# Sorted attention and expert layer: v sorted ahead of k, and the load of q heads 4 to 7 moved behind the k sort

## The chip, the cores and the metric

The kernel runs on one core of one Trainium2 chip. The metric is the device time of one execution in microseconds (us). A profile gives the span of the program on the core, about 2 us less than the device time. Ratios below come from runs of both kernels on the same chip, in the same rounds.

## The reference, cut to what matters

```python
P = sort_net                                   # [4, 8, 8, 8], five Sinkhorn steps
for _ in range(5):
    P = exp(P - max(P)); P = P / sum(P, -1); P = P / sum(P, -2)
k_sorted = einsum('bhij,bhjcd->bhicd', P, k_blocks)      # "sort" of k and v: 8 blocks mixed by P
v_sorted = einsum('bhij,bhjcd->bhicd', P, v_blocks)
attn = softmax(q_block @ k_sorted_block.T / 8)           # within each of the 8 blocks of 96
x = (attn @ v_sorted_block)                              # -> [3072, 512]
e = argmax(x @ w_gate + modality_bias)                   # one expert of 8 for each row
out = gate * (relu(x @ w1[e]) @ w2[e])
```

q, k and v are [4, 8, 768, 64] in fp32; the expert weights are [8, 512, 1024] and [8, 1024, 512].

## The kernel before

The 32 pairs of batch and head are worked in two groups of 16 pairs of rows. For each group k and v are brought to SBUF (GpSimd issues these loads, they cast fp32 to bf16), mixed by a 128 x 128 block matrix `bd` on TensorE (the sorts), and evacuated (copied out of TensorE's output buffers) by ScalarE and VectorE. q is loaded, *spread* (a copy that interleaves two heads), and transposed on TensorE. 32 units then follow, each with scores, exp and the product with v. Behind units 0 to 7 the rows go through a gate and are *scattered* by expert into a scratch table in HBM, and from unit 16 on the first expert's matmuls are mixed in, which read the scratch table through a transposed load (`xT`).

The loads at the start, in GpSimd's program order:

```python
load_q(0, 0, 2)
...                                   # cut: iota, identity
load_k(0, 0)
load_k(0, 1)
load_v(0)
load_q(0, 2, 2)
load_q(0, 4, 4)
...                                   # cut: constants
spread_q(0, 0, nc.gpsimd)
```

and the first group's sorts:

```python
kinds = [s_] + [m_] * 4 + [o_] + [m_] * 4 + ([m_] * 4 + [o_]) * 2 + [m_] * 4
g0 = jobs(0, kinds)                   # 10 jobs of k, then 14 of v
for f, g, x0, kd in g0[:10]:
    f(g, x0, kd)
load_k(1, 0)
load_k(1, 1)
home_map()                            # VectorE, then GpSimd: which expert is "home"
spread_q(0, 1, nc.gpsimd)             # q heads 2 and 3
gate_w()
for n, (f, g, x0, kd) in enumerate(g0[10:]):
    f(g, x0, kd)
    ...                               # cut: scores of units 0 and 1 in between
load_v(1)
spread_q(0, 2, nc.gpsimd)             # q heads 4 and 5
gate_bias()
prep_q(2); av(0); prep_q(3)
spread_q(0, 3, nc.gpsimd)             # q heads 6 and 7
load_q(1, 0, 4)
load_w(0, parts=(0,))
load_q(1, 4, 4)
load_w(0, parts=(1,))                 # last bulk load ahead of the experts
```

What an expert's first matmul stands on: eight scatters of `place(0)`, then the transposed load.

```python
ins = nc.gpsimd.indirect_dma_start(out=xs_dram, ..., in_=xt[:, t])       # 8 times, one queue
i1 = nc.sync.dma_start_transpose(out=xT_b[s % NX], in_=view)             # waits for all 8
nc.tensor.matmul(hp[:, f], w_at(...), xT_b[s % NX][:, c], ...)           # mL1
```

The softmax here doesn't subtract the row's maximum and nothing guards it: scores larger than these inputs give would overflow.

## Time and profile before

| | before |
|---|---|
| device time, median of the first 3 runs | 188.99 us (188.81 to 190.06) |
| span of the profile | 186.9 us |
| TensorE busy | 160.0 us, 86% |
| last packet of the bulk loads ends | 61.61 us |
| first expert matmul (`hp`) starts | 69.33 us |
| from there to the end | 117.6 us |

How to read it: the page's slices show which resource is full at what time, the chain of waits shows what released each step, the timeline gives single instructions with the idle time in front of them in brackets. Lines such as L365 are lines of the kernel; the changed kernel's are one or two lower. The packet times in this document are from the trace's record of DMA packets.

### The profile page before, as it was taken

Reading aid. Unit: us, or ns where it says so; the run is one execution under the profiler, and the core shown is the slowest. Engines: PE = TensorE matmul, PEld = TensorE weight load, DVE = VectorE, ACT = ScalarE, POOL = GpSimd, SP = SyncE. Lnnn points to the kernel's source line nnn. Section 1 sums busy time; section 2 is a strip of 40 time slices with the busy share of each in tenths; the row PEclk is TensorE's granted clock in tenths of the full one; section 3 lists DMA queues with packets and bytes.
Section 4 is the critical chain, followed back from the end, with each engine's and each line's share of the span. In section 5 each row is a group of like instructions: output and inputs, shape, how many; then the busy total and the mean of one; then the engine's idle time right before and its main releaser. Section 6 shows DMA issues by size and latency. Waiting matters only on the chain.

```text
span 186.9 us, 5311 instructions
## 1 busy us (share of the span) xinstructions
PE 160.0 (86%) x2116; PEld 121.0 (65%) x2127; DVE 101.5 (54%) x334; ACT 91.5 (49%) x147; POOL 83.7 (45%) x118
## 2 busy tenths in 40 slices
PE   6495597888499978999899999999999995999980
PEld 6484496766388966767648867658666664676430
DVE  4878677975557967848694657014723223132321
ACT  3134577766759875956467724532422321223120
POOL 7921288970085204455507744676522322206232
PEclk9969999999858999999999999999999999999999
DMA  3999999999999534999219532797469852002311
GB/s 45 208 217 210 193 211 216 224 206 218 211 203 221 159 60 64 189 184 287 70 26 123 186 102 77 128 242 192 132 129 202 169 145 71 24 36 109 119 56 56
DMA packets 30161, 27.67 MB, mean 148 GB/s; under 512 B 18831, under 2 KB 25775, under 8 KB 29872
## 3 DMA queue, kind: packets, MB, share of 16 engines
q0 software_dynamic: 11792, 23.10, 55.8%
q1 hardware_dynamic: 18336, 4.16, 14.0%
q8 instruction: 18, 0.29, 0.7%
q14 instruction: 15, 0.12, 0.2%
HBM read 27.35 MB, written 10.52 MB: 203 GB/s over the span
## 4 chain that ended last, share of the span: by engine, by line
PE 35%; DMA 23%; issue 21%; POOL 9%; DVE 8%; POOLq 2%; SPq 0%; DVEq 0%
PE hp L690 11%; DMA out_dram<-kvb,idg 11%; PE yp L713 9%; DMA kvb<-in_v_dram 9%; POOL xs_scratch L534 4%; POOL out_dram L704 4%; PE va L374 3%; PE op L436 3%; DVE xb L444 3%; PE gt L453 2%; PE sc L417 2%; PE lg L463 2%; DMA xs_scratch<-xb,dest 2%; DMA xT<-xs_scratch 2%; DVE v_sb L352 1%
## 5 line engine op out<-in xcount | busy, mean ns | idle before, releaser
L690 PE MATMUL hp<-xT,w 128*128 128x256 bf16 x384 | 46.4, 273 | 1.5 <-DMA xT<-xs_scratch 1.4
L534 POOL DMA_INDIRECT xs_scratch<-xb,dest x32 | 29.5, 922 | 34.4 <-issue 27.5
L704 POOL DMA_INDIRECT out_dram<-kvb,idg x25 | 24.6, 985 | 43.0 <-DVE kvb L702 16.8
L690 PEld LDWEIGHTS <-w 128*128 128x128 bf16 x384 | 36.3, 98 | 9.5 <-issue 1.4
L423 ACT ACTIVATE attnT<-sc 96x768 bf16<-96x768 f32 x32 | 25.9, 810 | 7.7 <-PE sc L417 7.3
L713 PE MATMUL yp<-w,hT 128*128 128x512 bf16 x90 | 21.9, 379 | 2.2 <-PEq L1009 1.9
L444 DVE TENSOR_TENSOR xb<-op,rs 96x512 bf16<-96x512 f32 x32 | 22.0, 686 | 1.1
L713 PE MATMUL yp<-w,qT 128*128 128x512 bf16 x91 | 22.3, 379 | 0.3
L700 ACT ACTIVATE kvb<-yp,idg 128x512 f32<-128x512 f32 x14 | 9.6, 687 | 22.9 <-PE yp L713 22.9
L702 DVE TENSOR_SCALAR kvb<-yp,idg 128x512 f32<-128x512 f32 x10 | 7.5, 751 | 20.0 <-PE yp L713 18.1
L713 PEld LDWEIGHTS <-hT 128*128 128x128 bf16 x96 | 9.0, 98 | 11.2 <-issue 2.1
L436 PE MATMUL op<-v_sb,attnT 96*128 96x65 bf16 x256 | 13.6, 197 | 2.9 <-DVE xb L444 2.4
L684 ACT ACTIVATE hT<-hp 128x512 bf16<-128x512 f32 x18 | 10.7, 596 | 10.8 <-PE hp L690 10.3
L684 ACT ACTIVATE qT<-hp 128x512 bf16<-128x512 f32 x16 | 9.3, 594 | 12.8 <-PE hp L690 12.2
L713 PEld LDWEIGHTS <-qT 128*128 128x128 bf16 x96 | 9.0, 98 | 9.3
L374 PE MATMUL va<-bd,kvb 128*128 128x128 bf16 x128 | 13.2, 261 | 1.5 <-DMA kvb<-in_v_dram 1.5
L374 PEld LDWEIGHTS <-kvb 128*128 128x128 bf16 x128 | 12.4, 200 | 1.7 <-DMA kvb<-in_v_dram 1.6
L352 ACT CAST kT<-ka 128x512 bf16<-128x512 f32 (+1 forms) x17 | 9.9, 640 | 6.9 <-PE ka L365 6.9
L436 PEld LDWEIGHTS <-attnT 96*128 96x128 bf16 x256 | 10.7, 100 | 3.9 <-DVE xb L444 2.8
L242 ACT COPY qT<-tq 128x768 bf16<-128x768 bf16 x14 | 11.1, 794 | 3.6 <-PE tq L236 3.5
L352 ACT CAST v_sb<-va 96x512 bf16<-96x512 f32 (+1 forms) x19 | 10.9, 613 | 3.8 <-PE va L374 3.4
L682 DVE TENSOR_SCALAR hT<-hp 128x512 bf16<-128x512 f32 x6 | 4.1, 692 | 14.4 <-PE hp L690 13.3
(182 smaller groups left out, 227.3 us busy)
## 6 DMA issues: line engine op xcount, KB each, us to landing
w<-in_moe_w_dram POOLq DMA_DIRECT2D x4, 1024.0 KB
kvb<-in_k_dram POOLq DMA_DIRECT2D x4, 768.0 KB
kvb<-in_v_dram POOLq DMA_DIRECT2D x2, 1536.0 KB
q_in<-in_q_dram POOLq DMA_DIRECT2D x4, 384.0 KB
xs_scratch<-zpad SPq DMA_DIRECT2D x3, 258.0 KB, 3.2
v_sb<-in_q_dram POOLq DMA_DIRECT2D x4, 192.0 KB
v_sb<-in_q_dram POOLq DMA_DIRECT2D x2, 384.0 KB
xs_scratch<-xb,dest POOLq DMA_INDIRECT x32
```

The costliest lines, as they stand in the source:

```text
L242: eng(qT, tq.pop(u).rearrange("p t (i r) -> p i t r", r=16))
L352: (nc.scalar.copy if pick(act, dve) else nc.vector.tensor_copy)(dst, src)
L374: nc.tensor.matmul(acc[:, z], v_cols[:, d0 + z], bd[g], start=True, stop=True)
L423: mark[0] = nc.scalar.activation(attnT[u % 2][:, 0:8 * BLK].rearrange("p (r f) -> p r f", r=2), sc_tiles.pop(u)[0:BLK, :, 0:4 * BLK], ACT. ...
L436: nc.tensor.matmul(ov[:, par, j], attnT[u % 2][:, c0:c0 + 128], v_sb[g][0:BLK, par * 64 + h * 8 + i, 0:D + 1], start=True, stop=True)
L444: nc.vector.tensor_tensor(xt[:, :, h * D:(h + 1) * D].rearrange("p (r j) d -> p r j d", r=2), ov[0:BLK, :, :, 0:D], rs.broadcast_to([BLK, ...
L534: ins = nc.gpsimd.indirect_dma_start(out=xs_dram, out_offset=bass.IndirectOffsetOnAxis(ap=dest[:, t:t + 1], axis=0), in_=xt.bitcast(I32)[: ...
L684: mark[0] = nc.scalar.activation(dst, src, ACT.Relu)
L690: nc.tensor.matmul(hp[:, f], w_at(s, c * F + (2 * j + f) * 128, 128), xT_b[s % NX][:, c], start=(c == 0), stop=(c == 3))
L700: nc.scalar.activation(dst, src, ACT.Copy, scale=gate)
L704: ins = nc.gpsimd.indirect_dma_start(out=out, out_offset=bass.IndirectOffsetOnAxis(ap=idg[:, t, 0:1], axis=0), in_=y, in_offset=None, boun ...
L713: nc.tensor.matmul(yp, hT_b[s % 2][:, fc, t * 128:(t + 1) * 128], w_at(s, 4 * F + fc * Dm, Dm), start=(fc == 0), stop=(fc == 7))
```

## The change

Intent: k lands early and v late, so that TensorE sorts k, pauses, and waits 1.5 us for v. With v first, the wide v matmuls run while k is still landing. The load of q heads 4 to 7 and the second group's loads are to go out only when the k sort is nearly over, so that no bulk load is under way there, and the spreads of heads 4 to 7 move to VectorE.

```diff
     load_q(0, 0, 2)
+    load_v(0)
     load_k(0, 0)
     load_k(0, 1)
-    load_v(0)
     load_q(0, 2, 2)
-    load_q(0, 4, 4)
 ...
+    for f, g, x0, kd in g0[10:]:
+        f(g, x0, kd)
+    home_map()
+    spread_q(0, 1, nc.gpsimd)
     for f, g, x0, kd in g0[:10]:
         f(g, x0, kd)
-    (second k loads, home_map, spread of heads 2 and 3, gate_w, v sort with scores 0 and 1 inside)
-    load_v(1)
-    spread_q(0, 2, nc.gpsimd)
+    load_q(0, 4, 4)
+    load_v(1)
+    gate_w()
+    prep_q(2); scores(0); expo(0); mod_T(); prep_q(3); scores(1); expo(1)
+    load_k(1, 0)
+    load_k(1, 1)
     gate_bias()
     av(0)
-    spread_q(0, 3, nc.gpsimd)
     load_q(1, 0, 4)
 ...
+    for hq in (2, 3):                      # in units 2 and 4, on VectorE
+        at1(2 * hq - 2, lambda hq: (spread_q(0, hq), use(dve=0.7)), hq)
```

(Cuts marked with "..."; the removed lines in brackets are summed up.)

More of the change, by code (lines that the diff above doesn't have):

```diff
@@ L772 @@
     g0 = jobs(0, kinds)
+    for f, g, x0, kd in g0[10:]:
+        f(g, x0, kd)
+    home_map()
+    spread_q(0, 1, nc.gpsimd)
     for f, g, x0, kd in g0[:10]:
         f(g, x0, kd)
+    load_q(0, 4, 4)
+    load_v(1)
+    gate_w()
+    use(dve=-busy[1], act=-busy[0])
+    prep_q(2)
+    scores(0)
+    expo(0)
+    mod_T()
+    prep_q(3)
+    scores(1)
+    expo(1)
     load_k(1, 0)
     load_k(1, 1)
-    home_map()
-    spread_q(0, 1, nc.gpsimd)
-    gate_w()
-    use(dve=-busy[1], act=-busy[0])
-    for n, (f, g, x0, kd) in enumerate(g0[10:]):
-        f(g, x0, kd)
-        if n == 1:
-            scores(0)
-            expo(0)
-            mod_T()
-        if n == 6:
-            scores(1)
-            expo(1)
-    load_v(1)
-    spread_q(0, 2, nc.gpsimd)
     gate_bias()
-    prep_q(2)
     av(0)
-    prep_q(3)
-    spread_q(0, 3, nc.gpsimd)
     load_q(1, 0, 4)
```

## The prediction

> **What bounds the kernel now.** I read the page's slices first, then the chain of waits, then the timeline and the windows of the stages that the change touches. The slices cut the 186.9 us span into 40 pieces of 4.67 us; each digit is a busy share in tenths:
>
> ```profile
> PE   6495597888499978999899999999999995999980
> POOL 7921288970085204455507744676522322206232
> PEclk9969999999858999999999999999999999999999
> DMA  3999999999999534999219532797469852002311
> ```
>
> The DMA row stands at 9 from slice 2 to slice 13, that is from about 5 us to 60 us: the loads of q, k, v and of the first expert's weights are one unbroken stream. The PE row is mostly 9 only from slice 16 on (70 us). So there are two halves: a front half in which the DMA stream is saturated, and a back half in which TensorE is. What joins them is in the chain of waits (start us, length us, what):
>
> ```profile
> 62.16 0.23 POOLq L641
> 62.39 3.39 DMA xs_scratch<-xb,dest
> 65.85 3.34 DMA xT<-xs_scratch
> 69.19 0.14 issue
> 69.33 1.05 PE hp L690 x8
> ```
>
> and in the two waits about it, the first of GpSimd over the whole span, the second of TensorE up to 69.4 us (us in total, times, longest):
>
> ```profile
> POOL xs_scratch L534 <- DMA w<-in_moe_w_dram: 2.6, 1, 2.6
> ...
> PE hp L690 <- DMA xT<-xs_scratch: 1.2, 1, 1.2
> ```
>
> The last of the eight scattered rows of the first group goes out only when the last bulk load (the second half of the first expert's weights) has landed; by the trace's landing records that is at 62.13 us. Then a scatter (3.39 us) and a transposed load (3.34 us) pass before the first expert matmul at 69.33. TensorE reached that matmul 1.2 us too early and waited. In the windows view TensorE is busy 59.8 of the 62.2 us from 69.3 to 131.5. So **the end of the kernel is the end of the bulk stream plus a constant**, as long as TensorE's own front half is no more than 1.2 us later than now.
>
> Inside the front half the change aims at these rows of the timeline (start, busy, engine, line, operation, and in brackets the idle time before and its releaser):
>
> ```profile
> 15.78 2.12 PE L365 MATMUL ka<-bd,kvb 128*64 128x64 bf16 x122 [0.90 <-DVE bd L292]
> 19.40 1.30 PE L365 MATMUL ka<-bd,kvb 128*64 128x64 bf16 x70 [1.50 <-issue]
> 22.21 0.93 PE L374 MATMUL va<-bd,kvb 128*128 128x128 bf16 x8 [1.51 <-DMA kvb<-in_v_dram]
> 25.23 1.60 POOL L127 COPY q_il<-v_sb 128x768 bf16<-128x768 bf16 x2 [0.29 <-DMA v_sb<-in_q_dram]
> 31.79 0.50 PE L236 MATMUL tq<-ident,q_il 128*128 128x128 bf16 x6
> ```
>
> The k sort is cut in two by 1.50 us in which TensorE waits for nothing that the profile names, and the v sort starts 1.51 us late because v lands at 22.16. The fourth row is GpSimd spreading q heads 2 and 3, the fifth the q transpose of head 4.
>
> **What the Trainium skill says.** (1) Runtime: NRT & Kernel Launch, section Instruction fetch mechanics: instructions come in 16 KiB blocks of 256 over a DMA queue, while the current ones run. The trace agrees: the instruction queue moved 18 packets and 0.29 MB, so 16 KiB each, and one of them ran from 17.11 to 18.08 us, in the middle of the bulk stream, just before the 1.50 us hole ended. I take the hole to be that fetch; it is inferred. (2) DMA: Bandwidth & Descriptors, section Latency and other measured facts: about 1 us to the first byte of a transfer issued by GpSimd. Here it is longer: the second expert's weights were issued at 72.52 us on a quiet queue and their first packet is at 74.06, and the first load of all was issued at 1.43 with a first packet at 3.03. I use 1.6 us. (3) GPSIMD Engine Reference, section 3.1, has GpSimd about two times slower than VectorE on elementwise work. Here one spread copy takes 0.80 us on GpSimd (1.60 for two) and 0.305 on VectorE (0.61 for two at 61.93 us), 2.6 times. (4) TensorE: Matmul & The Clock Gate, section on what is actually happening: an idle window of about 3.4 us halves the clock. The trace agrees in kind: the granted clock is 0.5 from 50.19 to 57.02, after a patchy stretch.
>
> **The change part by part.**
>
> *v ahead of k.* Bytes are the same, only the order differs: v lands where k did (14.5 us, in place of 22.2), k where v did. The sort can start on v as soon as the sort matrix is there (15.7 us, as now), so the 1.51 us wait for v goes. The block boundary that made the 1.50 us hole lies at the same place of TensorE's program, about its 447th instruction. The reordering puts 64 v matmuls ahead, so the boundary falls at the 58th of 192 k matmuls, some 24 us, when that fetch has long come: gain up to 1.5 us. But the sort is also held by evacuation. VectorE is in the home-expert chain till 18.56; then it has one wide copy (1.22) and four narrow ones (0.68 each) of v, and k's four after the four small instructions of the home map (0.85). Stepping through the order of both evacuating engines, I get v done on TensorE at 22.2, on VectorE at 23.1, the home map at 24.0, k evacuated at about 27.0. Today v, the second of the two, is evacuated at 30.0, with two units of scores inside; so the sort itself gains some 1 to 2 us.
>
> *Heads 4 to 7 of q behind the sort.* Today this load (two of 384 KB) follows heads 2 and 3 directly: in the packet records the small q packets run from 20.74 to 28.29, with heads 2 and 3 ending near 23.1. In the changed order GpSimd first does the home map, then the spread of heads 2 and 3, and only then issues the load. GpSimd: table ready 24.0, home map 2.2 us (22.69 to 24.93 today) to 26.2, spread 1.6 to 27.9. Issue at 27.9, first packet 1.6 later, at 29.5. Nothing else is in the queue: the next k and v loads stand behind it in GpSimd's program. So **the stream stands idle from about 23.1 to 29.5, 6.4 us**. The stream has no holes later in which to win this back: v, k, q and weights of the second group follow as today, 100% fed. Engines that lag today (heads 2 and 3 land between 22.96 and 25.11 on the 16) restart together, worth perhaps 0.5 us. Net 5.9 us later for everything behind it.
>
> *Spread of heads 4 to 7 on VectorE.* Two times 0.61 us go to VectorE, 3.2 us leave GpSimd. The copy time is hidden. But the first of them now waits for heads 4 to 7: 29.5, about 4 us of packets, about 1 to land: 34.5; the copy makes 35.2; the transpose of head 4 then runs at 35.2 in place of 31.79, 3.4 later, and VectorE is stuck before the evacuation of the unit ahead of it. All that the sort gained is lost in this wait, and TensorE idles from 31 to 35, which risks the half clock for one or two windows of 3.4 us, up to 1.7 us each.
>
> *Second group's v ahead of its k.* The program still sorts k first there. k was landed by 36 us; now it is behind q and v: about 29.5 + 4.4 + 7.5 + 7.5 + 1.4 = 50.3 for its second half (7.5 us for each 1.57 MB, as v took from 14.5 to 22.2). That half is first needed at about 46.9 today, 50.3 after the 3.4 shift: it just fits, or costs a microsecond.
>
> *The sum.* TensorE's own path reaches the first expert matmul at 68.0 + 3.4 plus nothing to 3.5 of clock: 71.4 to 75. The data for it come at 69.3 + 5.9 = 75.2. The later one counts. Behind it the program is unchanged and TensorE-bound, so the time is 188.99 + 5.9 = **194.9 us**.
>
> **The rivals.** *The hole is small or hidden:* if the loads go out earlier than I think (VectorE's copies finish sooner, the spread starts when q lands at 25.1), the idle time shrinks to some 5 us: 193.5. To be harmless it would have to be under the 1.2 us of slack. What speaks for the change is only that the sort runs without its two stalls of 1.5 us, which would give about 186.5 if the DMA stream were not the limit; the 1.2 us wait in front of the first expert matmul speaks against that, for TensorE is early already. *TensorE becomes the limit:* the wait of head 4, half clock and the late second k add up beyond 5.9; then 196 to 198. The fillers on ones_bf in units 2 to 7 speak against a long half clock. *The back half gives time back:* little, for its named waits on TensorE are 1.9 for a branch and under 2 us for the rest.
>
> **Range and chances.** From 192.0 (hole of 4 to 5 us, skew gone, a little regained) to 197.8 (6.4 plus a clock window and a late k). Faster by over 2% would need that no hole arises at all: 0.03. Within 2% (up to 192.8) needs a shift under 3.8 us: 0.13. Slower: 0.84.
>
> **What would show it.** Right: a DMA slice near 24 to 29 us that falls well below 9, q heads 4 to 7 issued near 28 us, the transposes of head 4 behind a VectorE spread near 35 us, the last weights landing near 68, the first expert matmul near 75 with TensorE waiting on the transposed load, and the same length from there to the end. The sort without holes at v and at its middle. Wrong: if the stream keeps at 9 there, or if the first expert matmul stays near 69.

## The result, and the profile after

| | before | after |
|---|---|---|
| device time, median of 4 runs | 188.90 us (188.13 to 190.06) | 197.62 us (196.90 to 199.09) |
| ratio | | 1.0466, 95% interval 1.0385 to 1.0548 |
| span of the profile | 186.9 us | 195.0 us |
| load stream idle, early | none | 23.99 to 29.69 us |
| head 4 transposed | 31.79 | 36.44 |
| last packet of the bulk loads ends | 61.61 | 68.98 |
| first expert matmul starts | 69.33 | 77.79 |
| from there to the end | 117.6 | 117.2 |

A ratio is the mean time of one kernel's fast runs over that of the other's fast runs of the same rounds, so it is not quite the ratio of the medians. The change makes the kernel 4.7% slower.

The same four rows of slices as in the prediction, of the changed kernel (one slice is now 4.88 us):

```profile
PE   6748973599998999899979999999999996999980
POOL 7800098931003740435631774376633232205232
PEclk9985996555555599999999999999999999999999
DMA  4999709999999946499712862479658863011311
```

The DMA row falls to 7 and 0 in slices 5 and 6 (19.5 to 29 us): the stream stops. The PE row falls to 3 in the next slice (slice 7, 29 to 34 us), and the granted clock is about half from slice 7 to 14. The timeline says who waits for whom there:

```profile
16.33 6.46 PE L373 MATMUL va<-bd,kvb 128*128 128x128 bf16 x64 [0.90 <-DVE bd L291]
...
22.72 3.51 PE L364 MATMUL ka<-bd,kvb 128*64 128x64 bf16 x186
...
26.63 1.57 POOL L127 COPY q_il<-v_sb 128x768 bf16<-128x768 bf16 x2
...
26.75 0.28 PE L364 MATMUL ka<-bd,kvb 128*64 128x64 bf16 x6 [0.51 <-issue]
...
28.16 1.57 POOL L120 DMA_DIRECT2D v_sb<-in_q_dram  x2
29.70 0.57 POOL L114 DMA_DIRECT2D kvb<-in_v_dram  x1
...
35.63 1.02 DVE L127 COPY q_il<-v_sb 128x768 bf16<-128x768 bf16 x2 [4.78 <-DMA v_sb<-in_q_dram]
...
36.44 0.82 PE L235 MATMUL tq<-ident,q_il 128*128 128x128 bf16 x6 [4.91 <-DVE q_il L127]
```

The two holes of 1.5 us are gone: v runs in one piece, k in one piece but for 0.51 us after its 186th matmul. But GpSimd is not at the load of heads 4 to 7 before 28.16 us, VectorE idles 4.78 us for that load, and TensorE 4.91 us for VectorE. In this profile TensorE comes to the first expert matmul last, at 77.79, without a wait for the transposed load, which was issued at 72.82. In the control run of the same kernel (below) it comes early and waits.

### The profile page after: what moved, and what is told of

Read it like the earlier page. It is cut to its first block, busy times and chain, and to the rows that moved or that the text cites. A ratio compares the mean times of both kernels' runs of the same rounds, so it can differ in the third digit from the quotient of the medians.

```text
span 195.0 us, 5310 instructions
## 1 busy us (share of the span) xinstructions
PE 169.7 (87%) x2116; PEld 129.1 (66%) x2127; DVE 102.5 (53%) x336; ACT 91.9 (47%) x149; POOL 80.4 (41%) x114
## 4 chain that ended last, share of the span: by engine, by line
PE 51%; issue 13%; DMA 13%; DVE 12%; POOL 7%; POOLq 2%; ACT 0%; DVEq 0%
PE hp L689 11%; DMA out_dram<-kvb,idg 10%; PE yp L712 9%; PE va L373 6%; PE op L435 4%; PE gt L452 4%; PE sc L416 4%; PE lg L462 4%; POOL out_dram L703 4%; DMA v_sb<-in_q_dram 3%; PE ka L364 3%; PE tq L235 3%; PE op L439 2%; DVE xb L443 1%; POOL v_sb L120 1%
## 5 line engine op out<-in xcount | busy, mean ns | idle before, releaser
L533 POOL DMA_INDIRECT xs_scratch<-xb,dest x32 | 29.5, 921 | 39.3 <-issue 19.0
L435 PE MATMUL op<-v_sb,attnT 96*128 96x65 bf16 x256 | 15.3, 209 | 1.1 <-DVE xb L443 1.1
L241 ACT COPY qT<-tq 128x768 bf16<-128x768 bf16 x13 | 10.3, 793 | 10.9 <-PE tq L235 10.8
L235 PE MATMUL tq<-ident,q_il 128*128 128x128 bf16 x96 | 9.4, 243 | 6.6 <-DVE q_il L127 4.9
L351 ACT CAST v_sb<-va 96x512 bf16<-96x512 f32 (+1 forms) x22 | 12.4, 615 | 5.2 <-PE va L373 4.6
L435 PEld LDWEIGHTS <-attnT 96*128 96x128 bf16 x256 | 12.3, 108 | 2.0 <-DVE xb L443 1.6
L416 PE MATMUL sc<-qT,kT 64*128 64x96 bf16 (+1 forms) x256 | 12.7, 228 | 0.9 <-ACT attnT L422 0.9
L373 PEld LDWEIGHTS <-kvb 128*128 128x128 bf16 x128 | 12.9, 190 | 0.9 <-issue 0.8
```

The source lines that it names most:

```text
L235: nc.tensor.transpose(tp[:, t], src[:, t], ident)
L351: (nc.scalar.copy if pick(act, dve) else nc.vector.tensor_copy)(dst, src)
L373: nc.tensor.matmul(acc[:, z], v_cols[:, d0 + z], bd[g], start=True, stop=True)
L416: nc.tensor.matmul(sc[0:m, par, j * BLK:(j + 1) * BLK], kT[g][rows, x0:x0 + m], qT[rows, i], start=True, stop=True)
L435: nc.tensor.matmul(ov[:, par, j], attnT[u % 2][:, c0:c0 + 128], v_sb[g][0:BLK, par * 64 + h * 8 + i, 0:D + 1], start=True, stop=True)
L533: ins = nc.gpsimd.indirect_dma_start(out=xs_dram, out_offset=bass.IndirectOffsetOnAxis(ap=dest[:, t:t + 1], axis=0), in_=xt.bitcast(I32)[: ...
```

## The experiments

Twelve runs were made, on three chips. The first chip ran even the kernel before at 208.93 to 213.50 us. Its profiles show TensorE pausing again and again for no reason that they name (often about 1 us, once 2.38 us in e4_k1_first), so its four times are not used; three of its kernels were repeated on the second chip and one on the third. (The medians on the first chip were 218.52, 215.86, 216.40 and 214.68 us for e1 to e4 against 213.25, with ratios of 1.0387, 1.0310 and 1.0213 for e1, e2 and e4 and none for e3.) On these the kernel before took 188.03 to 190.14 us in fast runs (up to 193.53 in those marked slow).

| run | what it is | chip | median us | ratio to before | stream idle, early | bulk loads end | first expert matmul |
|---|---|---|---|---|---|---|---|
| c_after | the changed kernel | third | 197.38 | 1.0422 (1.0370 to 1.0474) | 23.71 to 29.61 | 69.14 | 76.27 |
| e3b | before, only loads moved late | second | 196.54 | 1.0424 (1.0348 to 1.0500) | 23.81 to 28.19 | 67.93 | 74.37 |
| e2b | changed, TensorE kept busy | second | 198.03 | 1.0507 (1.0429 to 1.0585) | 24.03 to 29.41 | 69.14 | 76.21 |
| e4b | changed, second k ahead of v | third | 197.70 | 1.0446 (1.0401 to 1.0490) | 23.71 to 29.14 | 68.72 | 75.05 |
| e1b | changed, q 4 to 7 loaded early | second | 194.10 | 1.0189 (1.0079 to 1.0300, two fast runs) | 28.02 to 28.60 | 64.32 | 74.14 (a slow run) |
| e5 | e1b and second v issued early | second | 191.73 | 1.0046 (two fast runs) | none | 61.41 | 70.03 |
| e9 | e5, instructions shifted | third | 195.79 | 1.0248 (1.0183 to 1.0312) | none | 61.12 | 68.36 |
| e7 | before, last weights after the scatters | third | 195.28 | 1.0322 (1.0273 to 1.0371) | none | 72.27 | 73.50 |

The last three columns come from one profile each; that of e1b fell in the slow state.

### The control: the changed kernel again (c_after)

> The changed kernel itself, as a control beside the others of this call. All theories: ratio 1.04 to 1.055, load stream idle from 24 to 29.6 us, first expert matmul near 77 us.

Measured as expected. Its chain of waits across the joint of the two halves (start, length, what):

```profile
69.78 3.05 DMA xs_scratch<-xb,dest
72.85 0.04 issue
72.89 3.24 DMA xT<-xs_scratch
76.13 0.14 issue
76.27 1.64 PE hp L689 x8
```

This is the same chain as before, 7 us later: the eighth scatter at 69.78 in place of 62.39, the expert matmul at 76.27 in place of 69.33. TensorE waited 1.5 us for the transposed load here. From there to the end it took 120.0 us, 2.4 more than before. The windows about the joint show why. First the kernel before, then the control; the columns are the window and its length, busy us and count of TensorE, weight loads, VectorE, ScalarE and GpSimd, then the granted clock, the DMA share and GB/s:

```profile
62.50:69.30 6.80, 5.59 (x102) 5.16 (x101) 5.72 (x15) 6.12 (x10) 0.83 (x1) 1.00 0.31 67
69.30:76.10 6.80, 6.04 (x102) 5.11 (x102) 4.75 (x18) 3.62 (x7) 2.00 (x3) 1.00 0.50 73
```

```profile
69.50:76.30 6.80, 5.34 (x97) 4.93 (x94) 5.62 (x14) 5.86 (x10) 0.91 (x1) 1.00 0.36 85
76.30:83.10 6.80, 6.58 (x66) 5.35 (x68) 3.85 (x12) 2.02 (x4) 2.06 (x3) 0.52 0.52 77
```

In the 6.8 us after the joint the control was granted half the clock and got 66 matmuls done where the kernel before did 102. In the first profile of the changed kernel it was the other way round: half clock from 30.47 to 68.02 us, TensorE last at the joint, then full clock and 117.2 us to the end. Both ways end within 1.2 us of each other (195.0 and 196.2 us of span).

The profiles of the other runs agree. In c_after, e3b, e2b, e4b and e7 TensorE waited 1.33 to 2.67 us at the joint; each had 3.4 to 6.8 us of half clock starting within 2.6 us of the joint, and took 119.2 to 120.1 us from there to the end. In the kernel before, the first profile of the changed kernel and e5 the wait was 1.23 us or nothing; none had half clock there, and they took 117.2 to 117.6 us. This goes together in all eight; no run was made to test the wait alone.

### The loads alone, in the old order of sorts (e3_hole_only, e3b_hole_only)

Theory: the idle stretch of the load stream is the cause. Rival: the order of the sorts is.

```diff
     load_q(0, 2, 2)
-    load_q(0, 4, 4)
 ...
     for f, g, x0, kd in g0[:10]:
         f(g, x0, kd)
-    load_k(1, 0)
-    load_k(1, 1)
     home_map()
     spread_q(0, 1, nc.gpsimd)
+    load_q(0, 4, 4)
+    load_k(1, 0)
+    load_k(1, 1)
```

> The kernel before (k sorted first, spreads on GpSimd) with only the loads moved: q heads 4 to 7 and then the second k are issued behind GpSimd's spread of heads 2 and 3. Theory (idle stream): packets stop near 23.5 and start again near 28.5 us, the first expert matmul starts near 75 us, time 194.5 (193 to 196.5), nearly all of the loss. Rival (sorting v first is what costs): 189 to 190.5.

> Repeat of e3_hole_only. The kernel before with q heads 4 to 7 and the second k issued behind GpSimd's spread of heads 2 and 3. Theory: idle stretch from 23.9 to 28.3 us as on the first chip, first expert matmul near 75 us, ratio 1.025 to 1.04. Rival (sorting v first costs): ratio under 1.01.

On the second chip the ratio is 1.0424, as much as the whole change and a little over the 1.04 expected. The slices and the wait at the joint:

```profile
DMA  4999719999999934699313943399459763012311
```

```profile
PE hp L689 <- DMA xT<-xs_scratch: 2.4, 1, 2.4
```

k is sorted first here, the spreads are on GpSimd, and the loss is all there. TensorE waits 2.4 us for the transposed load: the stream is what is late. (The first chip's runs were mostly slow ones: 216.40 us against 213.25.)

### TensorE kept busy in the wait (e2_warm, e2b_warm)

Rival: it is the half clock in the front half that costs the time.

```diff
+        if u == 1:
+            for z in range(44):
+                nc.tensor.matmul(op[:, z % 2, 4 * (D + 1):512], ones_bf, kT[0][:, 0:512 - 4 * (D + 1)],
+                                 start=True, stop=True)
```

> The changed kernel plus 44 filler matmuls of 252 columns into a spare part of unit 1's output bank, so that TensorE is busy while it waits for head 4 (31 to 36 us). Rival (the half clock from 30.47 to 68.02 us is the main loss): the clock stays at 1.0, and the time falls to 191 to 193. Theory (the late load stream sets the end): the clock stays at 1.0, TensorE reaches the first expert matmul near 74 us and waits there for the transposed load until some 76.5, time 196 (195 to 197), a gain of about 1.4 us at most.

> Repeat of e2_warm. The changed kernel plus 44 filler matmuls during the wait for head 4. Theory (late load stream): last packet of the first weights stays near 69 us, first expert matmul near 76.5 us, waiting on the transposed load, ratio 1.035 to 1.045. Rival (half clock is the main loss): ratio 1.01 to 1.025.

The fillers did their work only in part: the granted clock was full from 34.42 to 58.32 us, then half again to 68.56, where the expectation had full clock throughout. But TensorE came to the joint ahead of the data, at 76.21 us as expected:

```profile
PE hp L693 <- DMA xT<-xs_scratch: 1.3, 1, 1.3
```

The time did not fall: the ratio, 1.0507, is even over the 1.035 to 1.045 expected. So the half clock of the front half, plain as it is in the first profile, is not what costs the time: with less of it the late stream takes its place.

### The second group's k ahead of its v (e4_k1_first, e4b_k1_first)

```diff
     load_q(0, 4, 4)
-    load_v(1)
+    load_k(1, 0)
+    load_k(1, 1)
     gate_w()
 ...
-    load_k(1, 0)
-    load_k(1, 1)
+    load_v(1)
     gate_bias()
```

> The changed kernel with the second group's k loaded ahead of its v, as before. Theory (idle stream): the last weights land at the same time, TensorE's front half is no limit by more than 1.5 us, time 197 (196 to 198). Rival (the late second k holds TensorE's front half): k lands near 43 in place of 50.7 us, time 193 to 195.

> Repeat of e4_k1_first on a chip that runs the kernel before at 189 us. The changed kernel with the second group's k loaded ahead of its v. Theory (idle stream sets the end): within 1 us of the changed kernel, ratio 1.04 to 1.05, first expert matmul not before 76 us. Rival (the late second k is a cause): 3 us faster than the changed kernel, ratio 1.025 to 1.035.

The ratio is 1.0446 beside the control's 1.0422 on the same chip: no gain, so the late second k is not a cause. The first expert matmul, expected not before 76 us, started at 75.05. TensorE is a little earlier, and waits longer:

```profile
PE hp L689 <- DMA xT<-xs_scratch: 2.5, 1, 2.5
```

### Heads 4 to 7 loaded early again (e1_q_early, e1b_q_early)

```diff
     load_q(0, 2, 2)
+    load_q(0, 4, 4)
 ...
-    load_q(0, 4, 4)
     load_v(1)
```

> The changed kernel with one thing undone: q heads 4 to 7 are again loaded right behind heads 2 and 3; v is still sorted first and the spreads stay on VectorE. Theory (the idle stretch of the load stream from 23.99 to 29.69 us is the cause): q's packets fill most of it, the stream stands idle some 1.5 us before the second v, head 4 is transposed near 31.5 us again, the first expert matmul starts near 71 us, time 190.5 (189.5 to 192). Rival (the order of the sorts, or the second k behind the second v, or the spreads on VectorE cost the time): stays above 195.

> Repeat of e1_q_early, whose chip ran even the kernel before at 209 to 213 us, with TensorE stopping and starting for no named reason. The changed kernel with q heads 4 to 7 loaded right behind heads 2 and 3. Theory (the idle stretch of the load stream): idle stretch about 1 us, head 4 transposed near 32 us, first expert matmul near 71 us, ratio to before 1.00 to 1.015. Rival (sort order, VectorE spreads or late second k): ratio above 1.035. Third: if the clock falls to half as it did on the first chip (28 to 83 us), TensorE's front half is the limit and the ratio lies between.

Undoing this one line takes back more than half of the loss: 1.0189 on the second chip, a little over the 1.015 expected, from two fast runs (191.50 and 193.33 us); the other two were slow (194.87 and 195.27). The profile is of the slowest of them. In it the stream ends at 64.32 us, but the granted clock is at half from 27.03 to 57.75 us and TensorE comes to the first expert matmul last, at 74.14 us for the 71 expected: the third possibility that the expectation named. What the rest of the loss in the fast runs consists of is therefore not shown. The profile also has a wait of 2.82 us in the k sort, like that of the next run. (On the first chip it was 218.52 us, slower than the other three; the clock was at half from 28.20 to 82.81 us there.)

### No idle stretch at all (e5_no_hole)

e1b, and the second v is issued ahead of the home map and the spread, as soon as the first v is sorted:

```diff
+    load_v(1)
     home_map()
     spread_q(0, 1, nc.gpsimd)
 ...
-    load_v(1)
     gate_w()
```

> As e1b, and the second v is issued ahead of GpSimd's home map and spread, as soon as TensorE is done with the first v, so that the load stream never stands idle; v is still sorted first. Theory: the stream ends where it did before, first expert matmul at 69 to 70 us, ratio 0.995 to 1.005: sorting v first neither gains nor loses, because the stream sets the end. Rival (the sort gains its two stalls of 1.5 us): ratio 0.985. Rival (the sort order costs): above 1.02.

The stream is unbroken (the slices below), it ends at 61.41 us as before (61.61), and the fast runs are 189.51 and 189.78 us; their mean over that of the six fast runs of before, 188.77, is 1.0046. With the idle stretch gone the loss is gone in these two runs, with v still sorted first. The other two, 193.69 and 195.54 us, fell in the slow state, with clocks of 0.901 and 0.889; no reason for them was found. And sorting v first brought nothing. The profile does not put that down to the stream alone: the transposed load landed at 69.23 us (69.19 before), and TensorE, held up in its k sort, took it up only at 70.03.

```profile
DMA  3999999999999464999209532599559752102311
```

The timeline shows what the change had in mind with the late loads:

```profile
21.87 3.53 PE L365 MATMUL ka<-bd,kvb 128*64 128x64 bf16 x186
28.46 0.28 PE L365 MATMUL ka<-bd,kvb 128*64 128x64 bf16 x6 [3.07 <-issue]
```

With bulk loads out at the end of the k sort, the wait after the 186th k matmul is 3.07 us; in the changed kernel, where the stream stands idle there, it is 0.51.

### The same with the instructions shifted (e9_no_hole_shift)

Is that wait the fetch of an instruction block? In TensorE's program of e5 the 186th k matmul is followed by instruction 703; the hole in the kernel before stood at 447, which is 256 earlier.

```diff
     spin(52)
+    for z in range(104):
+        r0 = (z % 2) * 64
+        nc.tensor.matmul(warm[r0:r0 + 64, 0, 0:64], ones_bf[:, 0:64], ones_bf[:, 0:64], start=True, stop=True)
```

> e5_no_hole plus 104 small matmuls (64 x 64) in TensorE's idle time after 6.8 us, which shift every later instruction by 208 places. Theory (the wait of 3.07 us after 186 k matmuls is the fetch of the block that starts at TensorE's 703rd instruction, delayed by bulk loads): the boundary now falls at the 82nd k matmul, its fetch was asked for some 6 us earlier, so no wait above 0.5 us there and none after the 186th; a new one of 0 to 2 us may stand at the transposes of head 3 (the 959th). Head 4 is transposed near 32 us in place of 33.5, ratio 0.995 to 1.01. Rival (the wait belongs to those k matmuls, say to an evacuation): it stays after the 186th.

```profile
22.03 3.61 PE L368 MATMUL ka<-bd,kvb 128*64 128x64 bf16 x192
...
28.88 0.50 PE L236 MATMUL tq<-ident,q_il 128*128 128x128 bf16 x3 [0.89 <-issue]
```

All 192 k matmuls now run with no such wait at the end, and the new one of 0.89 us stands in the middle of the transposes of head 3, at instruction 959 of this program, which is 447 + 2 * 256. So the wait belongs to a place in the program and not to the k sort, and it is long where bulk loads are out. The instruction queue's own packets agree: one of 16 KiB ends at 18.08 us in the kernel before, 25.38 in the changed kernel, 27.02 in e5 and 27.47 in e9, and TensorE's wait ends 1.3 to 1.4 us after it each time. The packet of the second boundary takes about 0.95 us with the stream idle and with it full; what differs is its start, 24.43 us in the changed kernel and 26.06 in e5. The first expert matmul, for which the eighth scatter and TensorE both wait again (1.6 us for the weights, 0.5 us for the transposed load), starts at 68.36 us, 1 us earlier than in the kernel before. Yet the time is worse, and this was not expected: from there to the end it takes 122.9 us in place of 117.6. Part of it is the branch that ends the common part:

```profile
PE yp L716 <- issue: 4.6, 1, 4.6
```

It costs 4.6 us here, 1.9 before. As every later instruction has moved by 208 places, I take it that the branch's target now lies worse in its block; that is left open. The rest is in the trace. Behind that wait the granted clock was half from 158.47 to 165.29 us. The first 24 matmuls after the branch, before and in e9:

```profile
158.00 1.89 PE L713 MATMUL yp<-w,hT 128*128 128x512 bf16 x8 [1.89 <-PEq L1009]
159.73 1.91 PE L690 MATMUL hp<-xT,w 128*128 128x256 bf16 x16
```

```profile
159.58 3.57 PE L716 MATMUL yp<-w,hT 128*128 128x512 bf16 x8 [4.62 <-issue]
162.94 3.06 PE L693 MATMUL hp<-xT,w 128*128 128x256 bf16 x16
```

The next matmuls start at 161.47 us before and at 165.84 in e9, so the 24 took 3.5 and 6.3 us. That makes 2.8 us, and the branch 2.7, of the 5.3.

### The last weights behind the scatters (e7_before_w_late)

If the scatter behind the bulk stream holds the experts, the second half of the weights, which is needed some 9 us later, could give way to it.

```diff
-    load_w(0, parts=(1,))
 ...
     at1(9, place, 0)
+    at1(9, lambda: load_w(0, parts=(1,)))
```

> The kernel before with one move: the second half of the first expert's weights is issued after the first group's eight scattered rows, not ahead of them. Theory (the end of the kernel hangs on the scatter that stands behind the bulk stream): the eighth scatter goes out near 60.2 us in place of 62.4, the transposed load lands near 66.5, TensorE reaches the first expert matmul at 68.0 without a wait, 1.2 us earlier than before, ratio 0.990 to 0.996. Rival (the stream is not what holds the first expert matmul): ratio 0.998 to 1.002.

A miss: ratio 1.0322. The scatters did come earlier (the eighth at 60.54), and the transposed load was issued at 63.12 in place of 65.85, but:

```profile
60.54 2.57 DMA xs_scratch<-xb,dest
63.10 0.02 issue
63.12 10.24 DMA xT<-xs_scratch
```

Beside the 1 MB of weights the transposed load took 10.24 us in place of 3.34. The first expert matmul starts at 73.50, and half clock follows there too (74.41 to 81.23 us). The wait in front of the scatter was taken away and came back in the next transfer, larger. No version that beats the kernel before was found.

## Why the prediction was right

**The idle stretch.** Predicted from about 23.1 to 29.5 us, since GpSimd spreads heads 2 and 3 before it issues heads 4 to 7. Measured 23.99 to 29.69 in the profile and 23.71 to 29.61 in the control. The stretch came out 5.7 us long, not 6.4, since heads 2 and 3 ended later. Each step of GpSimd's path was within 0.5 us: spread done at 28.2 for 27.9, issue at 28.16 for 27.9, first packet at 29.69 for 29.5. e3b shows that the late loads alone make the loss, and e5's two fast runs that it goes when the stretch goes.

**How far the stream comes late.** Predicted 5.9 us, measured 7.4 (the last bulk packet ends at 68.98 for 61.61). Heads 4 to 7 were given 5 us from first packet to landing and took 5.85 (29.69 to 35.54); this term was too small by about 1 us. The packets show why: the prediction let the stream restart at full rate, but of the 768-byte packets of this load only 108 started up to 31 us, in 1.3 us, where 259 started in the microsecond after it. By these numbers some 0.9 us (an estimate) went in the restart, and as much again in the control (129 packets in 1.4 us).

**The joint.** Predicted: the later of TensorE and the data counts, 75.2 us. Measured 77.79 in the profile, where TensorE was later, and 76.27 in the control, where the data were. That the scatter and the transposed load add a constant held: 6.5 us from the eighth scatter to the matmul in the control, 6.9 before.

**The clock.** This was the mis-sized term. The prediction gave it "one or two windows of 3.4 us" in the front half and nothing behind the joint. In the first profile the half clock lasted 37.6 us, and in the control TensorE's 1.5 us wait at the joint was followed by 6.83 us of half clock, right under the first expert matmuls, worth 2.4 us. "Behind it the program is unchanged and TensorE-bound" was right for the program and wrong for its pace. That, and the 1 us above, are most of the step from the predicted 194.9 to 197.6 us, still inside the range, but at its upper end (197.8; one of the four runs, 199.09 us, lies beyond it).

**What the sorts gain.** Predicted 1 to 2 us on TensorE, lost again in the wait for head 4. The first product with v starts at 29.46 us, 0.63 earlier than before. The block boundary that made the 1.50 us hole was where it was put, but the next one, 256 further, fell at the end of the k sort, which the prediction did not look at. Without a load under way it cost 0.51 us.

**The second k behind the second v.** Predicted to just fit. It landed at 50.7 us for 50.3 (the sum's 7.5 us for v is 7.7 by the times it names, 14.5 to 22.2), and was needed after 53 us; e4b shows no gain from an earlier one.

**The rivals.** "TensorE becomes the limit" was true of the one profile, "the hole is small or hidden" of none. e2b and the control show that the first of these is not needed for the loss.

## What to carry to other kernels

When the loads are one saturated stream and something late hangs on the end of it, moving a load behind compute costs its idle time in full (here 1.6 to 1.9 us more than that, in the changed kernel, the control and e3b): look for what the issuing engine has to do ahead of the issue, not only at what the load itself waits for. A gain on an engine that already waits at the next joint is worth nothing (e4b), and a wait there can be followed by a lower clock, so that it costs twice (c_after; e9 behind the branch). Before a transfer is let past another, ask what will run beside it.

## What the Trainium skill lacked or had wrong

- **Runtime: NRT & Kernel Launch, Instruction fetch mechanics.** It gives TensorE a buffer of 2048 instructions and calls the cost of a block boundary mostly hidden. The runs agree on the block of 256 (waits at instructions 447, 703 and 959), but TensorE had to wait for a block as early as its 447th instruction, and the wait was 0.51 us with the load stream idle, 1.50 and 3.07 us with bulk loads out. That the fetch starts later when bulk loads are out (26.06 us in e5, 24.43 in the changed kernel) is not on the page.
- **The same section, on branches.** It says a taken branch can stall on a fetch, with no size: the wait at one branch was 1.9 us before, 4.6 us when the program had shifted by 208 instructions (that a fetch makes either, and why they differ, is not shown).
- **TensorE: Matmul & The Clock Gate, on what is actually happening.** It has the clock return after some 3.4 us of sustained activity. In the first profile TensorE was busy for 24.56 of the 26 us from 43.3 to 69.3 us, with its many small matmuls, and stayed at half clock till 68.02 (at half clock the six transposes of head 4 took 0.82 us, at full clock before 0.50, in the rows shown). And the control had 6.83 us of half clock after a wait of only 1.5 us.
- **DMA: Bandwidth & Descriptors, Latency and other measured facts.** About 1 us to the first byte of a load issued by GpSimd; here 1.5 to 1.6 us (28.16 to 29.69, 1.43 to 3.03, 72.52 to 74.06).
- **No page** that I read has the cost of a transposed load beside a bulk load: 10.24 us in place of 3.34.
- **GPSIMD Engine Reference, section 3.1.** A factor of about two to VectorE for an fp32 add; for this bf16 copy it is 2.6 (0.80 us to 0.305) where VectorE makes two in 0.61 us; but the pair for heads 4 and 5 took VectorE 1.02 us in the changed kernel, a factor of about 1.5.
